# One batch-1 decode step (cached attention plus gated FFN): the rows of the down projection dealt to the partitions anew, with a part loaded by GpSimd

## The chip, the cores and the metric

The kernel runs on one core of a Trainium2 chip. The metric is the device time of one execution in microseconds (us), the median of several runs; lower is better. A profile of one further execution stands beside it. The engines are TensorE (PE, with weight loads as PEld), VectorE (DVE), ScalarE (ACT), GpSimd (POOL) and SyncE (SP). Sixteen transfer engines move data between HBM and the 128 partitions of SBUF; SP, ACT and POOL can issue transfers to them.

## The reference

One token's row `x` (576 wide) goes through a layer norm, and then through two branches whose results are added to `x`: attention over a cache of 16,384 keys with 32 heads of 128, and a feed-forward block with a gated GELU and 4,608 hidden values.

```python
x = A_x                                     # (1, 1, 576)
xn = layernorm(x)
q = (xn @ wq)                               # 32 heads x 128
scores = einsum("bhqd,bhkd->bhqk", q, k_cache) * 128 ** -0.5   # k_cache (1, 32, 16384, 128)
o = einsum("bhqk,bhkd->bhqd", softmax(scores), v_cache)
attention = o.reshape(1, 1, 4096) @ wo
h = gelu_tanh(xn @ w_gate) * (xn @ w_up)    # 4608 wide
return x + attention + h @ w_down
```

Everything is fp32. K and V are 8.4 MB per head each; with the weights the kernel reads 587.6 MB.

## The kernel before

Every large load is issued by SP, in program order, and each goes to all 128 partitions. Two SBUF slots (`kslot`) hold K tiles, one (`vslot`) holds a V tile, each 64 KB per partition. A load waits until its slot has been read by its last user.

Start: wq and the two FFN input matrices (w_gate, w_up) are loaded into the same slots. `project` multiplies the normalized row with one of them. The output columns are cut into four quarters, one for each group of 32 PSUM partitions, and into three chunks (`FB`, in columns) for the three PSUM banks; quarter q writes partitions 32q to 32q+31. In `ffn`, each of the 32 partitions of a quarter keeps its own share of the columns: a multiplication with the mask `same` (L176) and a sum (L179) leave 36 values per partition (`WD_T`) in `gu`. `ffn_act` turns them into `hT`, 128 partitions by 36 columns: partition p holds the hidden values 36p to 36p+35.

Middle: 32 heads. For head h, `qk` multiplies the K tile with the spread query (L215) and sums over 128 (L216) on VectorE; `softmax` works on 128 by 128 scores; `pv` multiplies with the V tile on TensorE (L236, 64 instructions), one head behind. SP's order is K of head h+1, then V of head h. The V of the last head goes to a `kslot`.

End: `load_rows` loads wd as 36 rows per partition in two pieces (`WD_PIECES`, 28 into the V slot `ta`, 8 into the K slot `tb`), and wo as 32 rows per partition in six pieces (`WO_PIECES` 16, 8, 4, 2, 1, 1; the first into `tb` behind wd, the others into `te`). A row is 576 values, 2,304 bytes. `add_out` multiplies one column of `hT` (wd) or `oT` (wo) with one such row across the partitions (L281): as two halves of 288, accumulated in PSUM, for wd and the first 24 rows of wo, as four quarters of 144 for the last 8 rows. After 28 rows of wo, VectorE adds both halves to `x2`, TensorE brings them into the quarters, and the last four rows follow. One copy and one store of 4 partitions by ACT's queue end the program.

GpSimd has no transfers before; it sets constants at the start.

Of the kernel before, what the change touches and what calls it, by code (L numbers as in the profile page):

```python
# [8 lines left out]
F32 = mybir.dt.float32  # L9
AF = mybir.ActivationFunctionType  # L10
ALU = mybir.AluOpType
AX = mybir.AxisListType

P = 128
H, SK, DH = 32, 16384, 128
D, DF = 576, 4608
# [3 lines left out]
DM = P * DJ  # L20
# [3 lines left out]
HD = H * DH  # L24
QG, QB = HD // 4, 512
QS = HD // 2
WD_T = DF // P
FG = DF // 4
FB = (11 * WD_T, 11 * WD_T, 10 * WD_T)
WO_T = HD // P  # L30
WD_PIECES = (28, 8)
WO_PIECES = (16, 8, 4, 2, 1, 1)
WO_A = 16
WO_Q = 8
QUART = D // 4
HG = 4
# [5 lines left out]
def kernel(ctx: ExitStack, tc: tile.TileContext, x, k_cache, v_cache, wq, wo, wg, wu, wd, out):  # L42
    nc = tc.nc
    cpool = ctx.enter_context(tc.tile_pool(name="cpool", bufs=1))
# [12 lines left out]
    wmain = {n: w[:DM].rearrange("(p j) f -> p (j f)", j=DJ) for n, w in (("q", wq), ("g", wg), ("u", wu))}  # L57
    wtail = {n: w[DM:].rearrange("d (s f) -> (d s) f", s=2) for n, w in (("q", wq), ("g", wg), ("u", wu))}
    wov = wo.rearrange("(p t) f -> p (t f)", t=WO_T)
    wdv = wd.rearrange("(p t) f -> p (t f)", t=WD_T)  # L60

    def kslot():
        return kpool.tile([P, R * DH], F32, tag="k", name="kslot")

    def vslot():
        return vpool.tile([P, R * DH], F32, tag="v", name="vslot")

    def load(dst, src):
        nc.sync.dma_start(dst, src)  # L69
        return dst  # L70

    ROW3 = 3 * DF
    wq_t, wg_t, mix = kslot(), kslot(), vslot()
    qt = load(wg_t[:, ROW3 : ROW3 + QS], wtail["q"])
    load(wq_t, wmain["q"])
    row3, tails, at = {}, {}, 0
# [2 lines left out]
        tails[n] = load(mix[:, at + DF : at + DF + DF // 2], wtail[n])  # L79
        at += DF + DF // 2  # L80

    xrow = mix[:1, ROW3 + FG : ROW3 + FG + D]
    nc.scalar.dma_start(xrow, xf)
    x2 = cpool.tile([P, HALF], F32, name="x2")
    nc.gpsimd.memset(x2, 0.0)
# [5 lines left out]
    ones = cpool.tile([P, P], F32, name="ones")  # L91
# [5 lines left out]
    same = cpool.tile([P, 32], F32, name="same")  # L97
# [14 lines left out]
    px = ps_s.tile([P, 512], F32, tag="sm", name="px")  # L112
    xm = xrow[:, :DM].rearrange("o (p j) -> o j p", j=DJ)
    for j in range(DJ):
        nc.tensor.matmul(px[:, j : j + 1], xm[:, j, :], ones[:1, :1], start=True, stop=True)
    xd = mix[:1, ROW3 + 2 * FG : ROW3 + 2 * FG + 2 * (D - DM)].rearrange("o (d s) -> o d s", s=2)
    nc.vector.tensor_copy(xd, xrow[:, DM:].unsqueeze(2).to_broadcast([1, D - DM, 2]))
    nc.tensor.matmul(px[:, DJ : DJ + 1], xd.rearrange("o d s -> o (d s)"), ones[:1, :1], start=True, stop=True)
    xp = cpool.tile([P, DJ + 1], F32, name="xp")
# [1 line left out]
    xnb = cpool.tile([P, DJ, 32], F32, name="xnb")  # L121
# [3 lines left out]
    xtb = cpool.tile([P, 2, 32], F32, name="xtb")  # L125
    nc.vector.tensor_copy(xtb, xt.unsqueeze(2).to_broadcast([P, 2, 32]))

    def project(steps, group, sizes):
        pg = ps_big.tile([P, 3, 512], F32, tag="pb", name="pg")
        for k, (j, rhs) in enumerate(steps):  # L130
            for b, size in enumerate(sizes):
                for q in range(4):
                    lo = q * group + sum(sizes[:b])
                    if j < DJ:
                        lhs = xnb[:, j, :]
                    else:
                        lhs = xtb[:, q // 2, :]
                        lo -= q // 2 * 2 * group
                    nc.tensor.matmul(pg[32 * q : 32 * q + 32, b, :size], lhs, rhs[:, lo : lo + size],  # L139
                                     start=k == 0, stop=k == len(steps) - 1)  # L140
        return pg

    steps = [(DJ, qt)] + [(j, wq_t[:, j * HD : (j + 1) * HD]) for j in range(DJ)]
    pq = project(steps, QG, (QB, QB))[:, :2, :]
    qrow = cpool.tile([P, QG], F32, name="qrow")
    nc.scalar.activation(qrow.rearrange("p (b f) -> p b f", f=QB), pq, AF.Copy)

# [2 lines left out]
    def q_spread(h):  # L150
        r = 32 * (h // (H // 4))
        lo = h % (H // 4) * DH
        pq = ps_s.tile([P, 512], F32, tag="sm", name="pq")
        nc.tensor.matmul(pq, ones[r : r + 1, :], qrow[r : r + 1, lo : lo + QH * DH], start=True, stop=True)  # L154
        return pq
# [4 lines left out]
        for i in range(QH):  # L160
            Q[h + i] = qs[:, i : i + 1, :]

    gu = cpool.tile([P, 2, WD_T], F32, name="gu")

    def ffn(which):
        n = "gu"[which]
        t = kslot() if which else wg_t
        steps = [(3, row3[n]), (DJ, tails[n])]
        load(t[:, :ROW3], wmain[n][:, :ROW3])
        steps += [(j, t[:, j * DF : (j + 1) * DF]) for j in range(DJ - 1)]  # L170
        pg = project(steps, FG, FB)
        gm = mix[:, ROW3 : ROW3 + FG].rearrange("p (m t) -> p m t", t=WD_T)
        at = 0
        for b, size in enumerate(FB):
            m = size // WD_T
            nc.vector.tensor_mul(gm[:, at : at + m, :], pg[:, b, :size].rearrange("p (m t) -> p m t", t=WD_T),  # L176
                                 same[:, at : at + m].unsqueeze(2).to_broadcast([P, m, WD_T]))
            at += m
        nc.vector.tensor_reduce(gu[:, which, :], gm.rearrange("p m t -> p t m"), axis=AX.X, op=ALU.add)  # L179

    ffn(0)
    ffn(1)

    hT = cpool.tile([P, WD_T], F32, name="hT")

    def ffn_act():
        g, u = gu[:, 0], gu[:, 1]
        t1 = cpool.tile([P, WD_T], F32, name="t1")
        tc.keep_in_program_order(nc.vector.tensor_mul(t1, g, g))
        tc.keep_in_program_order(nc.vector.tensor_scalar(t1, t1, 0.044715, 1.0, op0=ALU.mult, op1=ALU.add))  # L190
        tc.keep_in_program_order(nc.vector.tensor_mul(t1, t1, g))
        th = cpool.tile([P, WD_T], F32, name="th")
        nc.scalar.activation(th, t1, AF.Tanh, scale=0.7978845608028654)
        t2 = cpool.tile([P, WD_T], F32, name="t2")
        tc.keep_in_program_order(nc.vector.scalar_tensor_tensor(t2, th, 1.0, g, op0=ALU.add, op1=ALU.mult))
        tc.keep_in_program_order(nc.vector.scalar_tensor_tensor(hT, t2, 0.5, u, op0=ALU.mult, op1=ALU.mult))

# [51 lines left out]
    for h in range(H + 1):  # L249
        if h < H:  # L250
            KT[h], n = kslot(), R if h else SUB
            for i in range(0, R, n):
                load(KT[h][:, i * DH : (i + n) * DH], kv[h][:, i * DH : (i + n) * DH])
        if h > 0:
            VT[h - 1] = load(vslot() if h < H else kslot(), vv[h - 1])
        more = (h + 1) % QH == 0 and h + 1 < H
        pq = q_spread(h + 1) if more else None
        if h < H:
            for i in range(0, R, n):
                qk(h, i, n)  # L260
            KT.pop(h)
        if h == 0:
            ffn_act()
        if h > 0:
            pv(h - 1)
            if h % HG == 0:
                out_heads(h - HG)
        if more:
            q_take(h + 1, pq)
        if h < H:  # L270
            softmax(h)

    seen = set()
# [4 lines left out]
    def add_out(groups, lhs, w, last=False):  # L278
        n = D // len(groups)
        for i, g in enumerate(groups):  # L280
            nc.tensor.matmul(g, lhs, w[:, i * n : (i + 1) * n], start=id(g) not in seen, stop=last)  # L281
            seen.add(id(g))

    half = [[pairs[i][32 * (2 * i + j) : 32 * (2 * i + j) + 1, :HALF] for j in range(2)] for i in range(2)]
    quart = [acc4[32 * g : 32 * g + 1, :] for g in range(4)]

    def load_rows(t, at, src, lo, n):
        load(t[:, at * D : (at + n) * D], src[:, lo * D : (lo + n) * D])
        return [t[:, (at + j) * D : (at + j + 1) * D] for j in range(n)]

    ta, tb, te = vslot(), kslot(), kslot()
    a, b = WD_PIECES
    wd_rows = load_rows(ta, 0, wdv, 0, a) + load_rows(tb, 0, wdv, a, b)
    wo_rows, lo = [], 0
    for n in WO_PIECES:
        wo_rows += load_rows(tb, b + lo, wov, lo, n) if lo < WO_A else load_rows(te, lo - WO_A, wov, lo, n)
        lo += n
# [13 lines left out]

    for j, w in enumerate(wd_rows):
        add_out(half[j % 2], hT[:, j : j + 1], w)

    for j, w in enumerate(wo_rows):
        if j < WO_T - WO_Q:
            add_out(half[j % 2], oT[:, j : j + 1], w, last=j >= WO_T - WO_Q - 2)
            continue
        if j == WO_T - 4:
            nc.vector.tensor_add(x2[:64], x2[:64], PO[0][64:, :HALF])  # L320
            nc.vector.tensor_add(x2[:64], x2[:64], acc[:64, :HALF])
            for i, g in enumerate(quart):
                r, lo = 32 * (i // 2), i % 2 * QUART
                nc.tensor.matmul(g, ones[r : r + 1, :1], x2[r : r + 1, lo : lo + QUART], start=False, stop=False)
        add_out(quart, oT[:, j : j + 1], w, last=j == WO_T - 1)

    o4 = te[:, R * DH - 3 * HALF : R * DH - 3 * HALF + QUART]
# [30 lines left out]
```

## Time and profile before

| What | Value |
|---|---|
| Time, median of 3 runs | 1370.13 us (1369.86 to 1370.30) |
| The profiled execution's own time | 1370.16 us |
| Its span in the profile | 1368.3 us |
| VectorE busy | 1135.8 us (83%) |
| TensorE busy | 406.0 us (30%), weight loads 118.1 us |
| ScalarE, GpSimd busy | 36.5 us, 1.0 us |
| HBM read | 587.60 MB, 429 GB/s over the span |
| One `qk` of a full head on VectorE | L215 16.7 us mean, L216 16.7 us mean |
| First wd piece issued | 1308.00 us |
| wo pieces issued | from 1314.35 us, the second from about 1330 |

Times inside the profile count from the start of the span. The share of the transfer engines is a mean over all 16. A group's row names its line, engine, operation and tile, the shapes, the count, and then the busy time; in square brackets or behind the bar stands the idle time ahead of it and what ended it. The page counts packets by queue: q1 holds SP's loads, q10 ACT's, and q8 and q14 instruction loads.

### The profile page before, as it was taken

The page shows a single profiled execution, that of the slowest core. Times are in us where ns is not written, and L with a number is a line of the kernel's source. Part 1 is how long each engine was busy: PE and PEld are TensorE (multiplying, and loading weights), DVE is VectorE, ACT ScalarE, POOL GpSimd, SP SyncE. Part 2 cuts the span into 40 slices and gives each one's busy share as a digit, 9 for nine tenths or more (in the row PEclk, how much of TensorE's full clock was granted, in tenths as well). Part 3 has the DMA queues.
Part 4 walks back from the last instruction along what each step waited for, and adds up shares of the span by engine and source line. Part 5 has one row for each costly group of instructions (what it writes and reads, how often), then busy time and mean ns, then how long its engine had stood idle before and what let it go on. Part 6 is the DMA issues. An engine that isn't in the chain of part 4 may idle for free.

```text
span 1368.3 us, 6377 instructions
## 1 busy us (share of the span) xinstructions
PE 406.0 (30%) x2870; PEld 118.1 (9%) x2870; DVE 1135.8 (83%) x169; ACT 36.5 (3%) x126; POOL 1.0 (0%) x7
## 2 busy tenths in 40 slices
PE   4321233322311232323212332322213333221156
PEld 1110000100000000100000000100001000000012
DVE  1069999899888888898888888998888888988840
ACT  0000000000000000000000000000000000000000
POOL 0000000000000000000000000000000000000000
PEclk8775565565556556565566566565556555665577
DMA  9999999999999999999999999999999999999997
GB/s 404 440 425 450 430 429 430 430 435 432 437 435 429 431 430 439 432 432 435 431 436 433 433 431 430 435 432 439 435 430 430 431 432 437 438 435 428 429 428 336
DMA packets 11704, 588.00 MB, mean 430 GB/s; under 512 B 1303, under 2 KB 1309, under 8 KB 1694
## 3 DMA queue, kind: packets, MB, share of 16 engines
q1 hardware_dynamic: 11664, 587.60, 99.4%
q8 instruction: 22, 0.36, 0.1%
q14 instruction: 4, 0.03, 0.0%
q10 hardware_dynamic: 14, 0.01, 0.0%
HBM read 587.60 MB, written 0.00 MB: 429 GB/s over the span
## 4 chain that ended last, share of the span: by engine, by line
DMA 51%; DVE 46%; PE 2%; issue 0%; SPq 0%; ACT 0%; DVEq 0%
DMA kslot<-in_A_k_cache_dram 41%; DVE s L216 23%; DVE kslot L215 23%; DMA kslot<-in_A_v_cache_dram 3%; DMA kslot<-in_B_w_up_dram 3%; DMA kslot<-in_A_wo_dram 3%; DMA kslot<-in_A_wq_dram 2%; PE pg L139 1%; PE po L236 1%; DVE gu L179 0%; SPq L69 0%; PE pt L222 0%; DVE vslot L176 0%; DVE pm L220 0%; DVE nm L224 0%
## 5 line engine op out<-in xcount | busy, mean ns | idle before, releaser
L215 DVE TENSOR_TENSOR kslot<-kslot,qs 128x16384 f32<-128x16384 f32 (+1 forms) x33 | 551.3, 16705 | 88.4 <-DMA kslot<-in_A_k_cache_dram 86.9
L216 DVE TENSOR_REDUCE s<-kslot 128x128 f32<-128x16384 f32 (+1 forms) x33 | 551.2, 16703 | 3.3
L236 PE MATMUL po<-vslot,pe 128*16 128x512 f32 x1984 | 286.1, 741 | 645.0 <-DMA vslot<-in_A_v_cache_dram 645.0
L236 PEld LDWEIGHTS po<-vslot,pe 128*16 128x16 f32 x1984 | 67.3, 113 | 848.2 <-issue 848.2
L222 PE MATMUL pt<-ident,pm 128*1 128x128 f32 x32 | 11.9, 372 | 236.0 <-DVE pm L220 236.0
L176 DVE TENSOR_TENSOR vslot<-pg,same 128x396 f32<-128x396 f32 (+1 forms) x6 | 3.0, 552 | 69.1 <-PE pg L139 69.1
L139 PE MATMUL pg<-kslot,xnb 128*32 128x396 f32 (+2 forms) x208 | 23.6, 615 | 33.6 <-DMA kslot<-in_B_w_gate_dram 18.9
L228 ACT ACTIVATE nb<-pb 128x1 f32<-128x1 f32 x32 | 5.5, 171 | 812.4 <-PE pb L226 812.4
L320 DVE TENSOR_TENSOR x<-x,po 64x288 f32<-64x288 f32 x1 | 0.5, 457 | 30.8 <-PE po L281 30.8
L222 PEld LDWEIGHTS pt<-ident,pm 128*1 128x1 f32 x32 | 2.5, 79 | 259.4 <-DVE pm L220 218.5
L226 PE MATMUL pb<-nm,ones 1*128 1x1 f32 x64 | 18.1, 350 | 13.2 <-DVE nm L224 13.2
L224 DVE TENSOR_REDUCE nm<-pt 1x1 f32<-1x128 f32 x32 | 8.9, 278 | 14.9 <-PE pt L222 14.9
L226 PEld LDWEIGHTS pb<-nm,ones 1*128 1x128 f32 x64 | 15.8, 305 | 22.2 <-DVE nm L224 11.3
L154 PE MATMUL pq<-qrow,ones 1*128 1x512 f32 x16 | 15.6, 1073 | 0.0
L229 ACT ACTIVATE pe<-s,nb 128x128 f32<-128x128 f32 x32 | 12.8, 401 | 1.0
L302 DVE RECIPROCAL rl<-pl 128x32 f32<-128x32 f32 x1 | 0.4, 358 | 14.9 <-PE pl L300 14.9
L281 PE MATMUL acc<-kslot,oT 128*1 128x144 f32 (+1 forms) x112 | 10.5, 376 | 6.7 <-DMA kslot<-in_A_wo_dram 6.7
L139 PEld LDWEIGHTS pg<-kslot,xnb 128*32 128x32 f32 x208 | 7.1, 126 | 51.0 <-DMA kslot<-in_B_w_gate_dram 19.7
L241 ACT ACTIVATE o<-po 128x512 f32<-128x512 f32 x8 | 4.8, 597 | 222.0 <-PE po L236 222.0
L236 PE MATMUL po<-kslot,pe 128*16 128x512 f32 x64 | 9.6, 769 | 2.6 <-DMA kslot<-in_A_v_cache_dram 2.6
L281 PE MATMUL acc<-vslot,hT 128*1 128x288 f32 x56 | 8.6, 473 | 5.6 <-DMA vslot<-in_B_w_down_dram 5.6
L245 PE MATMUL pc<-same,o 128*128 128x4 f32 x64 | 8.4, 255 | 5.7 <-ACT o L241 5.7
(74 smaller groups left out, 109.9 us busy)
## 6 DMA issues: line engine op xcount, KB each, us to landing
kslot<-in_A_k_cache_dram SPq DMA_DIRECT2D x2, 4096.0 KB
vslot<-in_B_w_down_dram SPq DMA_DIRECT2D x1, 8064.0 KB
kslot<-in_B_w_gate_dram SPq DMA_DIRECT2D x1, 6912.0 KB, 54.0
kslot<-in_B_w_up_dram SPq DMA_DIRECT2D x1, 6912.0 KB
kslot<-in_A_wo_dram SPq DMA_DIRECT2D x1, 4608.0 KB, 39.2
vslot<-in_B_w_gate_dram SPq DMA_DIRECT2D x1, 2304.0 KB, 28.9
vslot<-in_B_w_up_dram SPq DMA_DIRECT2D x1, 2304.0 KB, 37.6
kslot<-in_B_w_down_dram SPq DMA_DIRECT2D x1, 2304.0 KB, 28.7
```

Source lines behind the costliest of these rows:

```text
L139: nc.tensor.matmul(pg[32 * q : 32 * q + 32, b, :size], lhs, rhs[:, lo : lo + size], start=k == 0, stop=k == len(steps) - 1)
L154: nc.tensor.matmul(pq, ones[r : r + 1, :], qrow[r : r + 1, lo : lo + QH * DH], start=True, stop=True)
L215: tc.keep_in_program_order(nc.vector.tensor_mul(blk, blk, Q[h].to_broadcast([P, n, DH])))
L216: nc.vector.tensor_reduce(S[h][:, i : i + n], blk, axis=AX.X, op=ALU.add)
L222: nc.tensor.transpose(pt[:1, :P], pm, ident)
L224: tc.keep_in_program_order(nc.vector.tensor_reduce(nm, pt[:1, :P], axis=AX.X, op=ALU.max, negate=True))
L226: nc.tensor.matmul(pb[:, :1], ones[:1, :], nm, start=True, stop=True)
L228: nc.scalar.activation(nb, pb[:, :1], AF.Copy, scale=SCALE)
L229: nc.scalar.activation(pe4, S.pop(h).rearrange("p (k s) -> p k s", s=4), AF.Exp, bias=nb, scale=SCALE, accum_out=lsum[:, h : h + 1])
L236: nc.tensor.matmul(PO[h // HG % 2][q : q + PW, :], pe[:, lo : lo + PW], vt[:, k * 512 : (k + 1) * 512], start=i == 0 and k < 4, stop=i == ...
L245: nc.tensor.matmul(pc[:, :HG], o4[:, j * DH : (j + 1) * DH], pick[:, j, :], start=j == 0, stop=j == 3)
L281: nc.tensor.matmul(g, lhs, w[:, i * n : (i + 1) * n], start=id(g) not in seen, stop=last)
```

## The change

wd has 4,608 rows. Before, partition p took the 36 rows 36p to 36p+35. Now each partition takes 33 (`WD_T`), rows 0 to 4,223 (`DX`), and the last 384 rows go, 12 more each (`WD_X`), to partitions 96 to 127 (`XP`).

- The 33 rows come in two SP pieces of 16 and 17. wo is cut into seven pieces, 11, 5, 8, 4, 2, 1, 1, with the first 11 in `tb`.
- The 12 extra rows come in four transfers that GpSimd issues. Transfer r goes to the 8 partitions 96+r, 100+r, ... 124+r, and each partition's 12 rows are read as two runs of 6 rows from two places of wd.
- Before, between and after these, GpSimd issues five transfers of 8-byte runs to 14, 8, 8, 8 and 10 partitions, into columns of `ta` that nothing reads.
- The FFN projections follow the new layout. Chunks are 15, 15 and 2 shares of 33 columns (495, 495, 66), with 384 columns more in the third chunk of the last quarter (450). Quarters begin at multiples of 1,056; where the tail's matrix (in two halves) is cut by a quarter's border, the matmul is split.
- `gu` and `hT` have 45 columns; for the last 12, partitions 96 to 127 get two more multiplications and two more sums per projection.
- The 12 extra rows are 12 further steps of `add_out` with 32 partitions, after the 33 others.
- The matmuls of `add_out` are kept in program order.

```diff
-WD_T = DF // P
-FG = DF // 4
-FB = (11 * WD_T, 11 * WD_T, 10 * WD_T)
+WD_T = 33
+WD_X = 12
+XP = 96
+DX = P * WD_T
+FT = WD_T + WD_X
+FG = 32 * WD_T
+FB = (15, 15, 2)
+FX = 32 * WD_X
-WD_PIECES = (28, 8)
-WO_PIECES = (16, 8, 4, 2, 1, 1)
-WO_A = 16
+WD_PIECES = (16, 17)
+WO_PIECES = (11, 5, 8, 4, 2, 1, 1)
+WO_A = 11
...
-    wdv = wd.rearrange("(p t) f -> p (t f)", t=WD_T)
+    wdv = wd[:DX].rearrange("(p t) f -> p (t f)", t=WD_T)
+    wdx = wd[DX:].rearrange("(s p t) f -> p s (t f)", s=2, t=WD_X // 2)
...
+        h = total // 2
...
-                    lo = q * group + sum(sizes[:b])
+                    lo = bases[q] + sum(sizes[q][:b])
+                    hi = lo + sizes[q][b]
                     if j < DJ:
-                        lhs = xnb[:, j, :]
+                        parts = [(xnb[:, j, :], lo, hi, 0)]
                     else:
-                        lhs = xtb[:, q // 2, :]
-                        lo -= q // 2 * 2 * group
-                    nc.tensor.matmul(pg[32 * q : 32 * q + 32, b, :size], lhs, rhs[:, lo : lo + size],
-                                     start=k == 0, stop=k == len(steps) - 1)
+                        parts = [(xtb[:, i, :], max(lo, i * h), min(hi, i * h + h), i * h) for i in range(2)]
+                    for lhs, a, e, o in parts:
+                        if a < e:
+                            nc.tensor.matmul(pg[32 * q : 32 * q + 32, b, a - lo : e - lo], lhs, rhs[:, a - o : e - o],
+                                             start=k == 0, stop=k == len(steps) - 1)
...
-        nc.vector.tensor_reduce(gu[:, which, :], gm.rearrange("p m t -> p t m"), axis=AX.X, op=ALU.add)
+        nc.vector.tensor_reduce(gu[:, which, :WD_T], gm.rearrange("p m t -> p t m"), axis=AX.X, op=ALU.add)
+        gx = mix[XP:, ROW3 + FG : ROW3 + FG + FX].rearrange("p (s m t) -> p s m t", s=2, t=WD_X // 2)
+        px = pg[XP:, 2, FB[2] * WD_T : FB[2] * WD_T + FX].rearrange("p (s m t) -> p s m t", s=2, t=WD_X // 2)
+        for i in range(2):
+            nc.vector.tensor_mul(gx[:, i], px[:, i], same[XP:, :].unsqueeze(2).to_broadcast([32, 32, WD_X // 2]))
+            nc.vector.tensor_reduce(gu[XP:, which, WD_T + i * WD_X // 2 : WD_T + (i + 1) * WD_X // 2],
+                                    gx[:, i].rearrange("p m t -> p t m"), axis=AX.X, op=ALU.add)
...
-            nc.tensor.matmul(g, lhs, w[:, i * n : (i + 1) * n], start=id(g) not in seen, stop=last)
+            tc.keep_in_program_order(nc.tensor.matmul(g, lhs, w[:, i * n : (i + 1) * n], start=id(g) not in seen, stop=last))
...
-    wd_rows = load_rows(ta, 0, wdv, 0, a) + load_rows(tb, 0, wdv, a, b)
+    wd_rows = load_rows(ta, 0, wdv, 0, a)
+    at = (a + WD_X) * D
+    halves = wd.rearrange("p (s f) -> p s f", s=2)
+    for r, n in enumerate((14, 8, 8, 8, 10)):
+        tc.keep_in_program_order(nc.gpsimd.dma_start(ta[0 : 4 * n : 4, at + 4 * r : at + 4 * r + 4], halves[:n, :, :2]))
+        if r < 4:
+            tc.keep_in_program_order(nc.gpsimd.dma_start(ta[XP + r : P : 4, a * D : at], wdx[r::4]))
+    wd_rows += load_rows(tb, 0, wdv, a, b)
+    wd_x = [ta[XP:, (a + j) * D : (a + j + 1) * D] for j in range(WD_X)]
...
     for j, w in enumerate(wd_rows):
         add_out(half[j % 2], hT[:, j : j + 1], w)
+    for j, w in enumerate(wd_x):
+        add_out(half[j % 2], hT[XP:, WD_T + j : WD_T + j + 1], w)
```

## The prediction

> **What bounds the kernel now.** I read the page from the top, then the chain of waits, then windows and timeline of the last 25 us, then the packets themselves.
>
> ```profile
> span 1368.3 us, 6377 instructions
> ...
> DMA  9999999999999999999999999999999999999997
> ...
> q1 hardware_dynamic: 11664, 587.60, 99.4%
> q8 instruction: 22, 0.36, 0.1%
> q14 instruction: 4, 0.03, 0.0%
> ```
>
> The transfer engines are busy in every slice but the last; the load queue alone fills 99.4% of them. VectorE (83%) has a 3.1 us gap per head. So the time is bytes over rate, plus what happens at the two ends. The chain ends in the loads of wo:
>
> ```profile
> 1318.24 9.66 PE po L236 x64
> 1329.71 35.08 DMA kslot<-in_A_wo_dram
> ```
>
> The windows of the end (us, busy time of each engine, granted clock, mean share of the 16 transfer engines, GB/s) show that the 16 do not stop together:
>
> ```profile
> 1356.00:1358.00 2.00, 2.00 (x24) 0.67 (x20) 0.00 (x0) 0.00 (x0) 0.00 (x0) 0.61 0.97 406
> 1358.00:1360.00 2.00, 2.00 (x40) 0.78 (x36) 0.00 (x0) 0.00 (x0) 0.00 (x0) 1.00 0.88 349
> 1360.00:1361.00 1.00, 1.00 (x24) 0.41 (x20) 0.00 (x0) 0.00 (x0) 0.00 (x0) 1.00 0.58 228
> 1361.00:1362.00 1.00, 0.61 (x12) 0.06 (x5) 0.32 (x1) 0.00 (x0) 0.00 (x0) 1.00 0.52 203
> 1362.00:1363.00 1.00, 0.98 (x32) 0.74 (x32) 0.58 (x2) 0.00 (x0) 0.00 (x0) 1.00 0.43 171
> 1363.00:1364.00 1.00, 1.00 (x32) 0.41 (x24) 0.00 (x0) 0.00 (x0) 0.00 (x0) 1.00 0.37 138
> 1364.00:1365.00 1.00, 0.70 (x21) 0.21 (x16) 0.00 (x0) 0.00 (x0) 0.00 (x0) 1.00 0.04 16
> ```
>
> From 1360 on about half are out of work, the last runs to 1364.4. The unused share from 1358 to 1364.36 is 0.24 + 0.42 + 0.48 + 0.57 + 0.63 + 0.32 = 2.66 us: **perfect evening gains no more than that**.
>
> The packet records tell who is late. On one engine a packet starts where the last ended, so 16 chains can be followed (a few swaps are possible). A 64 KB packet takes 2.42 us on all of them (27.07 bytes per ns). The 22 instruction packets of 16 KB visit eight engines in turn; each makes that engine's next load packet start 1.0 us late and run 0.5 us longer, 1.5 us in all. The eight have two or three such visits and their last load packets end at about 1362.5 (two) and 1363.7 to 1364.36 (six). The other eight end at 1359.1 to 1360.2, but for one at 1361.35, which takes two of the four 8 KB packets of q14 (0.97 us each). The engine that carries ScalarE's one-partition loads of x is one of the early eight. TensorE's end stands hard behind the landings:
>
> ```profile
> 1353.73 0.65 PE L281 MATMUL acc<-kslot,oT 128*1 128x288 f32 x2 [6.00 <-DMA kslot<-in_A_wo_dram]
> ...
> 1361.68 0.46 DVE L320 TENSOR_TENSOR x<-x,po 64x288 f32<-64x288 f32 x1 [30.80 <-PE po L281]
> ...
> 1363.46 1.06 PE L281 MATMUL acc<-kslot,oT 128*1 128x144 f32 x24
> ...
> 1364.83 0.42 PE L281 MATMUL acc<-kslot,oT 128*1 128x144 f32 x8 [0.30 <-DMA kslot<-in_A_wo_dram]
> ```
>
> The last row waited only 0.30 us for its load. Two things are nearly critical together: the latest engine, and TensorE's work from the 8-row piece of wo on.
>
> **The change part by part.** *Loads.* A row of wd in one partition is 2304 bytes: 0.0851 us of an engine. SP's pieces fall from 36 rows to 33; an engine serves 8 partitions (128 over 16), so each loses 24 rows, 2.04 us. The four GpSimd transfers bring 12 rows to 8 partitions each. Where a transfer of few partitions goes is seen in one row only: the output store of four partitions is four 576-byte packets of 31 to 34 ns that start within 60 ns and overlap, one engine per partition. By that, eight engines get four partitions, 48 rows, 4.08 us; net +2.04 us on eight, -2.04 us on eight. Fixed costs: two 9216-byte packets (0.351 us each) against one of 18432 (0.689) make 0.013 us a packet. The seventh piece of wo adds 8 packets, 0.10; the GpSimd transfers 8, 0.10; nine completion marks of about 0.012 with the 8-byte packets, 0.15. So +2.36 us on the eight that get the rows, -1.8 on the others. What a GpSimd packet costs no row shows. Lower bound: its bytes, 0.51 us (ScalarE's 1152-byte packets cost their engine 49 ns, close to the bytes' 43). Upper bound: the instruction packet's 1.5 us per 16 KB, 1.27 us for 13,824 bytes, 6 us more per engine. I take the lower: like ScalarE's, these move data from HBM to SBUF.
>
> *Which eight.* No row shows it. If the early ones: these end at 1361.5 to 1362.6, the one with two q14 packets at 1363.7; the late ones at 1361.9 to 1362.55. The last landing moves from 1364.36 to 1363.7: **-0.65 us**. If late ones are among them: 1364.36 + 2.36 = 1366.7, **+2.36**. I take the early ones, on an assumption that only the sizes in the diff support: that each GpSimd transfer takes the next engines in line, as many as it has partitions. Then 14, 8, 8, 8, 10 and four times 8 make 80, five rounds of 16, each real transfer begins 16 places after the last, and all four meet the same eight engines, as many as each group has. The Trainium skill (DMA: Bandwidth & Descriptors, section "Why a DMA increments its semaphore by 16 and not by 1") says that such a transfer takes consecutive engines from a cursor that moves on, but also that some direct copies from GpSimd are spread one partition per engine from engine 0, whatever went before. By the first the small transfers steer and the sum is -0.65; by the second they steer nothing, and it could be +2.36 (second rival). No run so far shows either.
>
> *GpSimd's queue.* Nine transfers, with nothing behind them but the end of the program. The first waits for the V slot, as SP's first wd piece does (issued 1308.00). The last waits for the first one's completion. The rows are needed after SP's 33, landed near 1340. Even 2.5 us for each of nine (the store's whole wait at the end) is 23 us, 1331: covered. Without cover, TensorE would stand before wo.
>
> *SP's queue.* The same waits on slots; its last one-row piece now waits for the first wd piece (about 1329): covered until 1362; only the end stands behind it.
>
> *Projections.* Four column quarters run side by side, so a step lasts as its widest: 495+495+450 = 1440 columns for 396+396+360 = 1152, a quarter more.
>
> ```profile
> 59.59 8.13 PE L139 MATMUL pg<-kslot,xnb 128*32 128x396 f32 x72 [18.88 <-DMA kslot<-in_B_w_gate_dram]
> ...
> 76.05 6.01 PE L139 MATMUL pg<-kslot,xnb 128*32 128x396 f32 x72 [2.58 <-DMA kslot<-in_B_w_up_dram]
> ```
>
> That is +1.5 to 2.0 us each, and four small VectorE operations each, 1.3 us by the rows of L176 and L179 scaled to 192 columns. K of head 1 (issued about 82) and V of head 0 (85.8) go out 2 to 4 us later, but the engines hold K of head 0 until 92.7 and K of head 1 until 112. VectorE starts head 0 3 us later; K of head 2, issued 120.7, then about 124, is needed at 131. Hidden; without cover, 3 us.
>
> *TensorE's end.* wd costs 45 rows for 36, 9 x 0.243 = 2.2 us, in stretches where TensorE waited for loads (6.00 us before 1353.73). wo comes as 11, 5, 8 for 16, 8, so TensorE is idle some 3 us before the 8-row piece. Rows took 0.48 us at clock 0.50 (1353.7 to 1357.5) and 0.243 at 1.00. The 8 rows landed at 1358.67 and would at 1358.0: at full clock they are done by 1360.6 and the landing decides, -0.65; at half clock they end near 1362.3 and the last row starts at 1365.1, +0.3. The Trainium skill (TensorE: Matmul & The Clock Gate, "Part 1: The HAM clock gate (the "warmup" mystery)") gives an idle window of about 3.4 us as what halves the clock; by that 3 us is just too short and the sum has no term here. The trace does not bear it out to the letter: its clock record falls at 1272.24, 2.5 us after TensorE stopped at 1269.8. I take most of the rows at full clock, +0.15.
>
> Sum: 1368.3 - 0.65 + 0.15 = 1367.8 span. The profiled execution took 1370.16, 1.86 outside its span, and lies within 0.03 of the median 1370.13: **1369.6 us**.
>
> **Rivals.** *All even and clock held*: the q14 packets visit other engines, or all wo rows run warm. For it: packet visits hang on code that has changed. Last landing 1362.6: 1370.13 - 1.8 = 1368.3. *The rows fall on late engines* (the other side): one engine with three instruction visits among the eight decides it. For it: a first transfer of 14 sets the start, and where zero lies no row tells; 8 of 16 engines are wrong. Against: the arithmetic above. Price +2.36 by the landing, to +3.3 where TensorE's clock has fallen too: 1372.5 to 1373.4. *TensorE's clock*: half clock for the 8 rows eats the gain, 1370.4. For it: the clock fell after 2.5 us idle at 1272. Against: the idle stretch is about 3 us. *GpSimd packets as dear as instruction packets*: 1362.6 + 6.0 = 1368.6, +4.3: 1374.4. Against: ScalarE's small packets are not.
>
> **How the numbers follow.** Forecast 0.38 (its own range 1368.8 to 1370.2), all even 0.12, TensorE's clock 0.10, late engines 0.36, dear packets 0.04. The range 1368.1 to 1373.3 leaves out the dear packets and the upper edge of the late engines. 0.2% (2.74 us) is about what a measurement of this kernel can tell from no change. Faster than 1367.39 would need more than the 2.66 us of perfect evening: 0.03 for what I may have missed. Slower than 1372.87: 0.26 of the late engines' 0.36 and the dear packets' 0.04, 0.30. The rest, 0.67.
>
> **What would show it.** In the windows of the last 6 us the transfer share should stay near 1 to about 1361 and then fall within 2 us; a share near 0.5 from 1358 to 1366 would be the late engines, and the forecast wrong. The four GpSimd transfers should land before 1331. The clock at the 8-row piece of wo, and the wait ahead of the last row (over 0.30: the landing decides; none: TensorE), tell the third rival. SP's first waits should still end before the engines run dry: a first-100-us share below today's would break the cover of the projections. 64 KB packets should still take 2.42 us.

## The result: 1375.56 us, 5.5 us slower, and the profile after

| | Before | After |
|---|---|---|
| Time, median (range) | 1370.04 us (1369.86 to 1370.30) | 1375.56 us (1375.30 to 1375.92, 6 runs) |
| Ratio to before, 95% interval | | 1.0040 [1.0030, 1.0051] |
| The profiled execution's own time / span | 1370.16 / 1368.3 us | 1375.92 / 1374.1 us |
| Last load packet ends | 1364.36 us | 1369.94 us |
| Last matmul ends | 1365.25 us | 1371.04 us |

The forecast was 1369.6 with a range to 1373.3: wrong in sign and outside its range. Last landing (+5.58), last matmul (+5.79) and span (+5.8) moved together, so the loss is in the loads of the end. The head of the page of the changed kernel, and the end of its chain of waits (start, length, what was waited for):

```profile
span 1374.1 us, 6485 instructions
...
DMA  9999999999999999999999999999999999999997
...
q1 hardware_dynamic: 11808, 586.72, 99.2%
q0 software_dynamic: 352, 0.89, 0.2%
```

```profile
1317.16 8.97 PE po L253 x64
1326.53 38.23 DMA kslot<-in_A_wo_dram
```

The transfer engines are as busy as before, with the same bytes, but the last wait on wo is 3.15 us longer (38.23 for 35.08). Busy for longer with the same bytes means slower packets. The windows say when (us, busy time of PE, PEld, DVE, ACT and POOL, clock, transfer share, GB/s). First the kernel before, then the changed kernel:

```profile
1310.00:1320.00 10.00, 2.72 (x15) 1.05 (x19) 4.51 (x3) 0.67 (x3) 0.00 (x0) 0.66 1.01 435
1320.00:1330.00 10.00, 9.15 (x70) 2.99 (x62) 0.09 (x1) 0.77 (x2) 0.00 (x0) 0.83 1.02 440
1330.00:1340.00 10.00, 3.39 (x26) 1.34 (x30) 0.75 (x3) 0.20 (x1) 0.00 (x0) 0.51 0.94 403
1340.00:1350.00 10.00, 7.73 (x124) 2.78 (x116) 0.00 (x0) 0.00 (x0) 0.00 (x0) 0.97 1.00 429
```

```profile
1310.00:1320.00 10.00, 3.79 (x19) 1.33 (x23) 1.34 (x3) 0.66 (x3) 0.61 (x2) 0.50 0.98 340
1320.00:1330.00 10.00, 7.78 (x64) 2.87 (x56) 0.84 (x3) 0.97 (x3) 0.00 (x0) 0.95 1.03 346
1330.00:1340.00 10.00, 6.91 (x64) 2.05 (x64) 0.00 (x0) 0.00 (x0) 0.00 (x0) 0.66 1.02 359
1340.00:1350.00 10.00, 1.51 (x16) 0.52 (x20) 0.00 (x0) 0.00 (x0) 0.00 (x0) 0.57 0.94 345
...
1356.00:1358.00 2.00, 2.00 (x36) 0.68 (x32) 0.00 (x0) 0.00 (x0) 0.00 (x0) 1.00 1.00 430
...
1365.00:1366.00 1.00, 1.00 (x16) 0.37 (x12) 0.00 (x0) 0.00 (x0) 0.00 (x0) 0.68 0.73 290
1366.00:1368.00 2.00, 2.00 (x20) 0.66 (x16) 0.00 (x0) 0.00 (x0) 0.00 (x0) 0.50 0.22 88
1368.00:1369.00 1.00, 1.00 (x24) 0.68 (x20) 0.58 (x2) 0.00 (x0) 0.00 (x0) 0.61 0.12 46
1369.00:1370.00 1.00, 1.00 (x32) 0.44 (x28) 0.32 (x1) 0.00 (x0) 0.00 (x0) 1.00 0.11 41
```

For forty microseconds the share is about 1 and the rate 340 to 359 GB/s, where the kernel before moved 403 to 440 in the same windows. By 1356 the rate is back (430). From 1366 to 1370 a share of 0.22 to 0.11 says that some two to four of the 16 engines still run.

The packet records show the same packet by packet. The unhindered length of each size is that of a run in which nothing slowed it:

| Packet | Unhindered | Before, mean | After, mean (range) |
|---|---|---|---|
| 65,536 (K, V after 1290) | 2418 ns | 2422.6 | 2466 (2418 to 3489) |
| 39,168 (wd, 17 rows) | 1448 | – | 1785 (1448 to 2382) |
| 36,864 (wd, 16 rows) | 1364 | – | 1702 (1364 to 2619) |
| 25,344 (wo, 11 rows) | 940 | – | 1042 (940 to 1707) |
| 13,824 (GpSimd's) | 516 | – | 678 (516 to 939) |
| 18,432 | 686 | 690.7 | 686 |

With eight packets of each wd and wo size per engine and 8.6 of 65,536 this is 8 x (337 + 338 + 102) ns + 8.6 x 48 ns = 6.6 us per engine, on engines with extra rows and without alike, as far as the chains can be told apart. Packets are long only while GpSimd's are under way (1311 to 1346), but for one that meets an instruction packet.

GpSimd issued without trouble (start, length, idle time ahead):

```profile
1305.42 0.70 POOL L314 DMA_DIRECT2D vslot<-in_B_w_down_dram  x1 [1303.84 <-PE po L253]
...
1309.48 0.56 POOL L316 DMA_DIRECT2D vslot<-in_B_w_down_dram  x1
1316.23 0.57 POOL L314 DMA_DIRECT2D vslot<-in_B_w_down_dram  x1 [6.18 <-DMA vslot<-in_B_w_down_dram]
```

The end of TensorE (the last rows of wo) shows a second effect:

```profile
1364.81 0.41 PE L298 MATMUL acc<-kslot,oT 128*1 128x288 f32 x2 [3.21 <-DMA kslot<-in_A_wo_dram]
...
1367.62 0.70 PE L298 MATMUL acc<-kslot,oT 128*1 128x288 f32 x2
...
1369.88 1.16 PE L298 MATMUL acc<-kslot,oT 128*1 128x144 f32 x32
```

TensorE waited 3.21 us for the 8-row piece; soon the clock fell to 0.50 and a matmul took 0.70 us for 0.41. The last four rows then ran without a wait.

### The profile page after: what moved, and what is told of

Its sections match the earlier page's. It is cut to its first block, busy times and chain, and to the rows that moved or that the text cites. A ratio compares the mean times of both kernels' runs of the same rounds, so it can differ in the third digit from the quotient of the medians.

```text
span 1374.1 us, 6485 instructions
## 1 busy us (share of the span) xinstructions
PE 416.8 (30%) x2910; PEld 123.1 (9%) x2910; DVE 1138.5 (83%) x178; ACT 36.5 (3%) x126; POOL 6.2 (0%) x16
## 4 chain that ended last, share of the span: by engine, by line
DVE 48%; DMA 45%; PE 4%; another core or an unknown queue 1%; issue 1%; ACT 0%; SPq 0%; DVEq 0%
DMA kslot<-in_A_k_cache_dram 37%; DVE s L233 24%; DVE kslot L232 24%; DMA kslot<-in_A_v_cache_dram 3%; PE pg L149 3%; DMA kslot<-in_A_wo_dram 3%; DMA kslot<-in_A_wq_dram 2%; PE po L253 1%; PE acc L298 0%; PE pt L239 0%; DVE gu L190 0%; DVE pm L237 0%; DVE vslot L187 0%; DVE nm L241 0%
## 5 line engine op out<-in xcount | busy, mean ns | idle before, releaser
L187 DVE TENSOR_TENSOR vslot<-pg,same 128x495 f32<-128x495 f32 (+1 forms) x6 | 2.8, 519 | 74.1 <-PE pg L149 74.1
L149 PE MATMUL pg<-kslot,xnb 128*32 128x495 f32 (+3 forms) x208 | 29.1, 643 | 28.7 <-DMA kslot<-in_B_w_gate_dram 17.0
L298 PE MATMUL acc<-vslot,hT 128*1 128x288 f32 (+1 forms) x56 | 10.0, 523 | 2.6 <-DMA vslot<-in_B_w_down_dram 2.6
```

Of the source, the lines that this page charges most:

```text
L149: nc.tensor.matmul(pg[32 * q : 32 * q + 32, b, a - lo : e - lo], lhs, rhs[:, a - o : e - o], start=k == 0, stop=k == len(steps) - 1)
L298: tc.keep_in_program_order(nc.tensor.matmul(g, lhs, w[:, i * n : (i + 1) * n], start=id(g) not in seen, stop=last))
```

## The experiments

Three theories stood against each other: (a) the rows fall on engines that were late anyway; (b) GpSimd's transfers are dear in themselves; (c) the place where the rows are written slows all loads. All kernels here compute the whole result. The first four shared 24 runs of before (1370.20), the next four 24 (1370.09), the next three 13 (1370.08), the last 11 (1370.06).

**data_only: without the five small transfers.**

```diff
-    for r, n in enumerate((14, 8, 8, 8, 10)):
-        tc.keep_in_program_order(nc.gpsimd.dma_start(ta[0 : 4 * n : 4, at + 4 * r : at + 4 * r + 4], halves[:n, :, :2]))
-        if r < 4:
-            tc.keep_in_program_order(nc.gpsimd.dma_start(ta[XP + r : P : 4, a * D : at], wdx[r::4]))
+    for r in range(4):
+        tc.keep_in_program_order(nc.gpsimd.dma_start(ta[XP + r : P : 4, a * D : at], wdx[r::4]))
```

> The changed kernel without its five small transfers; the four GpSimd transfers of the extra rows stay. In the changed kernel's trace load packets on every engine are stretched while the 13,824-byte GpSimd packets are in flight, and only then. Theory A (the rows' own GpSimd packets cost it, by their queue or by where they write): the transfer rate between 1310 and 1350 still falls to about 350 GB/s while they move; if they now take another set of eight engines, the last landing is up to 3 us earlier; 1371 to 1375. Theory B (the small transfers and their completion marks cost it): the rate stays near 430 and the time is 1369 to 1371.

Measured: 1371.48 us (1371.22 to 1372.08), ratio 1.0010 [1.0000, 1.0019]. Now the four transfers alternate between two groups of eight engines, and the records contrast them inside one kernel: packets of the first (starting near 1310 to 1315) take up to 1081 ns and of the third (1320 to 1327) up to 894; of the second (1316 to 1319) and fourth (from 1327.9) 516 to 534. The same rows at the same partitions cost their bytes' price from one eight and more from the other. That speaks against (b) and for (c).

**sp_four: the four transfers issued by SP, GpSimd does nothing.** In place of the GpSimd loop:

```diff
+    for r in range(4):
+        load(ta[XP + r : P : 4, a * D : at], wdx[r::4])
```

> The same four transfers of eight partitions, issued by SP behind the first wd piece; nothing from GpSimd, no small transfers. Theory A1 (GpSimd's queue is what is dear): no stretched packets, 1368 to 1370.5, depending on which eight engines SP's transfers take. Theory A2 (the destination is what is dear: partitions 96 to 127 are written by engines that otherwise write other partitions): the same stretch as with GpSimd, 1372 to 1375. Theory B (small transfers): as A1.

Measured: 1376.55 us (1374.24 to 1377.07), ratio 1.0043 [1.0028, 1.0058]: as slow without GpSimd, so (b) falls. Nine in ten of the 13,824-byte packets take over 0.9 us (mean 1022 ns, longest 1119): twice 516. Of the 128 packets of 39,168 bytes 31 take 2.7 to 3.1 us, about twice 1.448, 18 lie between, and 79 keep 1.448. Windows of this kernel:

```profile
1310.00:1320.00 10.00, 6.10 (x31) 1.83 (x35) 1.25 (x3) 0.67 (x3) 0.00 (x0) 0.51 1.02 437
1320.00:1330.00 10.00, 6.24 (x56) 2.63 (x44) 0.84 (x3) 0.97 (x3) 0.00 (x0) 0.83 1.09 244
1330.00:1340.00 10.00, 5.67 (x64) 1.73 (x64) 0.00 (x0) 0.00 (x0) 0.00 (x0) 0.83 0.89 312
1340.00:1350.00 10.00, 3.18 (x28) 0.99 (x32) 0.00 (x0) 0.00 (x0) 0.00 (x0) 0.51 0.98 423
```

The rate falls to 244 GB/s at a full share just while these packets run (1321 to 1334).

**deal_one: the rows in one SP transfer to the 32 partitions.** In place of the GpSimd loop:

```diff
+    load(ta[XP:, a * D : at], wdx)
```

> The new dealing with the extra rows in one SP transfer to partitions 96 to 127, two partitions to each engine if it is spread over all 16; so no shift between the engines and nothing from GpSimd. All theories but A2: the projections, the seven pieces of wo and TensorE's extra rows are hidden, the last landing is where it was, 1370 to 1370.6. A2: packets stretched for some microseconds, 1372 to 1374.

Measured: 1373.46 us (1372.84 to 1374.65), ratio 1.0025 [1.0015, 1.0035]. The packets are as long (mean 1026 ns), 233 GB/s from 1320 to 1330. By the chains they now lie on all 16 engines, about four each, so no engine has more rows than before; with (a) out of the way, 1373.46 - 1366.67 = 6.8 us over the kernel before at the same slot offset (pad_224 below) is left for (c). The changed kernel less gp_low is 6.8 us too (below), but with packets of another length on eight engines, so that the two agree so closely is in part chance.

**small_only: the kernel before with the five small transfers alone.**

```diff
+    for r, n in enumerate((14, 8, 8, 8, 10)):
+        tc.keep_in_program_order(nc.gpsimd.dma_start(ta[0 : 4 * n : 4, at + 4 * r : at + 4 * r + 4], halves[:n, :, :2]))
```

> The kernel before with the five small GpSimd transfers alone, rows dealt as before. Theory B: 3 to 6 us more, 1373 to 1376. Theory A: under 0.6 us, about 1370.3, with no stretched packets but at the small packets themselves.

Measured: 1370.30 us (1370.16 to 1370.49), ratio 1.0001 [0.9991, 1.0010]. The tiny transfers cost nothing that can be told.

**sp_low: the same rows on partitions 0 to 31, by SP.**

```diff
-XP = 96
+XP = 0
+XE = XP + 32
...
+    for r in range(4):
+        load(ta[XP + r : XE : 4, a * D : at], wdx[r::4])
```

`FT`, `hT` and the twelve steps stay; the 384 columns of the projections go to the first quarter, where a matmul with zeros opens the accumulation and the two stretches of columns follow.

> The new dealing with the extra rows on partitions 0 to 31 for 96 to 127, in four SP transfers of eight partitions; nothing from GpSimd. Where SP's transfers of eight partitions to 96 to 127 ran at half rate (1040 ns for 516) and doubled other engines' packets, theory A2 says that each engine writes the partitions it always serves at full rate, and that two engines share one path when one writes the other's partitions. If SP's eight engines serve partitions 0 to 63, no packet is stretched here (13,824 bytes in 516 ns, 39,168 in 1448), the late engines end 2 us sooner, the early ones 2.3 later: the time is 1365.5 to 1367.5 with the shorter 64 KB packets (2418 ns) that all kernels of the new layout show. Rival A3, any extra transfer of few partitions is dear wherever it writes: stretched packets as before, 1372 to 1376.

Measured: 1368.32 us (1367.29 to 1368.61), ratio 0.9986 [0.9976, 0.9995]. Every 13,824-byte packet takes 516 ns. The windows of this kernel:

```profile
1320.00:1330.00 10.00, 8.12 (x72) 3.35 (x68) 0.84 (x3) 0.97 (x3) 0.00 (x0) 0.84 1.00 432
1330.00:1340.00 10.00, 5.32 (x56) 1.49 (x48) 0.00 (x0) 0.00 (x0) 0.00 (x0) 0.67 0.94 405
```

The same transfers, rows and issuing engine as in sp_four, 8.2 us apart: only the partitions differ, with the projections that lead to them. This settles (c) for SP. What is left of (a) is seen too: the engines that carry rows and take three instruction packets end at 1362.31 and 1362.43, those with three and no rows at 1358.7 to 1359.0.

**gp_low: the same by GpSimd, each transfer followed by a small one of 8 partitions.**

```diff
+        tc.keep_in_program_order(nc.gpsimd.dma_start(ta[XP + r : XE : 4, a * D : at], wdx[r::4]))
+        tc.keep_in_program_order(nc.gpsimd.dma_start(ta[0:32:4, at + 4 * r : at + 4 * r + 4], halves[:8, :, :2]))
```

> The same rows on partitions 0 to 31, issued by GpSimd, each of the four transfers followed by a small one of eight partitions, so that all four fall on the same eight engines. A2: no stretch beyond the packets' own switching, within 1.5 us of the SP version, 1365.5 to 1369. Theory A1 (GpSimd's queue is dear in itself): stretched load packets between 1310 and 1350 on all engines, 3 us or more above the SP version.

Measured: 1368.77 us (1368.22 to 1369.76), ratio 0.9989 [0.9980, 0.9999]. All 64 packets take 516 ns. Windows of this kernel:

```profile
1320.00:1330.00 10.00, 8.12 (x96) 3.47 (x88) 0.84 (x3) 0.97 (x3) 0.00 (x0) 1.00 1.03 441
1330.00:1340.00 10.00, 1.47 (x27) 0.44 (x22) 0.00 (x0) 0.00 (x0) 0.00 (x0) 0.79 0.95 406
```

With GpSimd as issuer, and with the small transfers, the median is 0.45 us over SP's. The last landings differ by 0.36 us (1362.79 and 1362.43), and the runs of the two overlap, so a cost of the issuer is small at most.

**pad_224 and after_pad_32: a hidden gain.** The larger constants of the changed kernel move the K and V slots in SBUF: they began at byte 27,680 of a partition, 32 past a multiple of 256, and begin at 27,904, a multiple of 256. One kernel gives the kernel before this offset by an unused tile that is set to zero, the other takes it away from the changed kernel in the same way.

```diff
+    pad = cpool.tile([P, 56], F32, name="pad")   # before
...
+    pad = cpool.tile([P, 8], F32, name="pad")    # after
```

> The kernel before with a constant tile of 224 bytes per partition more, so that the K and V slots begin where they do in the changed kernel (SBUF offset 27,904 per partition, a multiple of 256, for 27,680, 32 above a multiple of 64). All kernels of the new layout show 64 KB packets of 2418 ns for 2420 to 2428. If the offset is the reason: 512 packets per engine times 4.6 ns, 2.4 us less, 1367.5 to 1368.2. If it is something else in the new layout: 1370.0 to 1370.4.

> The changed kernel with 32 bytes more per partition ahead of the slots (offset 27,936, again 32 above a multiple of 64). If the offset shortens the packets: 64 KB packets of 2420 to 2428 ns again and about 2.4 us more than the changed kernel, 1377.5 to 1378.5. Otherwise 1375.3 to 1375.9.

Measured: pad_224 1366.67 us (1366.46 to 1366.96), ratio 0.9975 [0.9965, 0.9984]; after_pad_32 1378.84 us (1378.61 to 1380.12), ratio 1.0065 [1.0050, 1.0080]. The offset is worth 3.4 us before and 3.3 after. At equal offset the change costs 1378.84 - 1370.09 = 8.75 us at the old one and 1375.56 - 1366.67 = 8.89 at the new. After 1290 every 64 KB packet takes 2418 ns in pad_224, in the kernel before 2419 to 2428 (mean 2422.6).

**who: which engines take instruction packets.** pad_224 with eight tiny SP loads to 1, 2, ... 8 partitions, each with its own packet size, so that an engine is known by the sizes that it carries.

```diff
+    for k in range(1, 9):
+        n = 22 + k
+        load(ta[0 : 4 * k : 4, at : at + n], wd[:k, :n])
+        at += n
```

> A reading, not a timing: the kernel before at the slots' better offset, with eight tiny SP loads more behind the first wd piece, of 1, 2, 3 ... 8 partitions and of a size of their own (92 to 120 bytes a partition), so that the packet records tell which chain is the first engine, the second and so on. If the eight engines that SP's transfers of eight partitions take are all early ones, none of the eight chains takes an instruction packet of 16 KB; the version with the rows on partitions 0 to 31 ended with two engines late, so I expect that two of the eight take them. SP's waits on its completion counters will cost a few microseconds: 1367 to 1373.

Measured, in a single run: 1371.4 us; the engines ran dry for 2.4 to 6.6 us near 1330 while SP issued these loads. The load of k partitions goes to the first k engines. As far as the chains can be told apart, engines 0 to 4 and 7 take no instruction packets, while 5 and 6 take two or three; the other six late ones then lie among 8 to 15. So the early eight are not eight in line: any eight in line include a late engine.

**sp_64 and sp_32: the other two places.** sp_low with another `XP`.

```diff
-XP = 0
+XP = 64    # or 32
```

> The extra rows on partitions 64 to 95 for 0 to 31, by the same SP transfers, nothing else changed. Theory A2 (two engines share one path where one writes partitions that the other serves): as on 96 to 127, half rate (13,824 bytes in about 1040 ns) and stretched wd packets, 1374 to 1377. Rival A4 (only the last quarter is slow, or the earlier version's layout): full rate, 1367.5 to 1369.

> The same on partitions 32 to 63. Theory A2, with engine i of the first eight serving 4i to 4i+3 and 32+4i to 32+4i+3: full rate, 516 ns, as on 0 to 31, 1367.5 to 1369. Rival A4' (only the first quarter is fast): half rate, 1374 to 1377.

Measured: sp_64 1377.54 us (1375.45 to 1378.83), ratio 1.0053 [1.0038, 1.0068]; sp_32 1368.73 us (1367.51 to 1372.22), ratio 0.9992 [0.9982, 1.0001]. The 13,824-byte packets: mean 1029 ns on 64 to 95, all 516 on 32 to 63. Windows of sp_64:

```profile
1320.00:1330.00 10.00, 7.25 (x64) 2.70 (x54) 0.84 (x3) 0.97 (x3) 0.00 (x0) 0.97 1.08 253
1330.00:1340.00 10.00, 6.31 (x64) 1.89 (x64) 0.00 (x0) 0.00 (x0) 0.00 (x0) 0.66 0.95 256
```

Upper half of the partitions slow, lower half not. The Trainium skill ("SBUF — State Buffer", section "Door 1: The DMA port swizzle (why `[64,N]` ≈ `[32,N]`)") says that eight partitions share one of 16 ports, 0 to 63 on eight of them and 64 to 127 on the other eight; "DMA: Bandwidth & Descriptors" (section "The descriptor swizzle") that a 128-partition transfer gives each engine one port, engines 0 to 7 the lower partitions. The four places agree: where engines 0 to 7 write the lower half, nothing slows; where they write the upper half, two engines write one port, and packets take 1022 to 1029 ns for 516. The records don't name ports, so that it is the port is an inference; that it hangs on engine and partition together is shown, by the four places and by data_only.

**four_engines: the rows where they cost nothing.** If this is so, rows should go to engines without instruction packets, on partitions of their own: 0 to 15 for engines 0 to 3. sp_low with 35 rows for all and 8 more for these, at the good offset.

```diff
-WD_T = 33
-WD_X = 12
-XE = XP + 32
+WD_T = 35
+WD_X = 8
+XE = XP + 16
...
-WD_PIECES = (16, 17)
-WO_PIECES = (11, 5, 8, 4, 2, 1, 1)
+WD_PIECES = (20, 15)
+WO_PIECES = (13, 3, 8, 4, 2, 1, 1)
```

> Slots at offset 27,904 as in pad_224; each row block of wd keeps 35 rows for all 128 partitions and gives partitions 0 to 15 eight rows more, by four SP transfers of 4 partitions, one for each of the engines 0 to 3, which take no instruction packets and serve these partitions. Theory (engines that write partitions of their own keep their rate, the two- and three-visit engines set the last landing): those lose 8 rows of 2 KB for each partition, 0.68 us by the price in the prediction, engines 0 to 3 gain 24 rows net, 2.04 us, on ends 4 us earlier; no packet stretched (13,824-byte packets absent, the 39,168-byte ones' successors at their bytes' price); 1365.8 to 1366.5 against pad_224's 1366.67. Rival, TensorE's half clock at the end decides by now: last landing earlier by 0.5 to 0.7 us, but the time stays at 1366.5 to 1368. Rival, the shared path costs also where the engine writes its own partitions: 1370 or more.

Measured: 1366.13 us (1365.91 to 1366.22, 7 runs), ratio 0.9971 [0.9959, 0.9982]: the lowest median of the study, 3.9 us under before and 0.54 under pad_224, whose own runs began at 1366.46. Load packets keep their unhindered lengths but for the few that meet an instruction packet. The last landing is 1360.47, where pad_224 has 1361.25: 0.78 earlier for the 0.68 expected. The timeline of this kernel's last row:

```profile
1360.84 0.42 PE L309 MATMUL acc<-kslot,oT 128*1 128x144 f32 x8 [0.28 <-DMA kslot<-in_A_wo_dram]
```

It waited 0.28 us for its load, at full clock: the landing decides.

## Why the prediction was wrong

The 5.5 us come out as: offset of the slots -3.4 (pad_224), rows on eight engines in line that include late ones +2.1 (gp_low less pad_224), packets slowed at the upper partitions and what follows from them +6.8 (after less gp_low). The offset was not in the prediction, the late engines were its second rival, the slowed packets were missing.

By the last landings of the profiled executions the three terms are -3.1, +1.5 and +7.2, 5.6 together. So the 2.1 is not late engines alone. In gp_low TensorE waited 3.84 us for the 8-row piece and then worked at half clock, and its last matmul ends 2.10 us after the last landing, where pad_224 has 0.81 and the changed kernel 1.10. That execution is the slowest of its ten. A window of gp_low, clock 0.50:

```profile
1360.00:1361.00 1.00, 1.00 (x12) 0.29 (x8) 0.00 (x0) 0.00 (x0) 0.00 (x0) 0.50 0.14 55
```

- **Loads, "I take the lower: like ScalarE's, these move data from HBM to SBUF".** This step failed. A packet was priced by its bytes, whatever partition it writes and whichever engine carries it. In gp_low the price was right to the nanosecond (516 ns, 0.51 us forecast): GpSimd's packets are not dear. At partitions 96 to 127 they took 678, and made others longer: 6.6 us per engine, a term that the sum lacked. "GpSimd packets as dear as instruction packets" came near in time (1374.4) by luck, with a mechanism that sp_four and gp_low refute.
- **The price of rows**, 4.08 us between an engine with and one without: sp_low shows 3.3 to 3.7 between engines with three visits (1362.31 to 1362.43 against 1358.73 to 1359.00). Right in kind, a little large. The packet sums do not close fully: for the late engine 2.36 + 6.6 + 8 x 0.162 for its own rows - 3.1 (landing of pad_224 against before) = 7.2, and its landing moved by 5.58. The chains of that stretch cannot all be told apart, and the rest stays open.
- **Which eight.** The arithmetic of places held: of the small transfers' packets the engines with rows carry one each and the others five, just what eight places in line give when the count runs on through 14, 8, 8, 8, 8, 8, 8, 8, 10. So the Trainium skill's rule of a cursor that moves on, weighed there, agrees with the trace; all transfers starting at engine 0 does not. What failed is "if the early ones": the early eight are not in line (who), and the late-engines rival came true for two engines (in the changed kernel they end at 1369.74 and 1369.94, all others by 1367.13).
- **GpSimd's queue**: nine issues of 0.56 to 0.70 us, the last 6.18 us after the one before, all out by 1316.8. The extra rows landed by 1346.3, not 1331. By then SP's wd pieces were still landing (39,168-byte packets start until 1346.5), so the cover was thin, but it held.
- **Projections**: the step over w_gate took 10.34 us for 8.13, 2.2 us more for the 1.5 to 2.0 forecast, and was hidden: the first 120 us moved 405, 439 and 444 GB/s, for 404, 438 and 445.

```profile
59.03 10.34 PE L149 MATMUL pg<-kslot,xnb 128*32 128x495 f32 x72 [16.98 <-DMA kslot<-in_B_w_gate_dram]
```

- **TensorE's end.** "Most of the rows at full clock" failed: after a wait of 3.21 us most of the 8 rows ran at half clock. The last landing was so late that this cost only some 0.2 to 0.3 us: from the last landing to the last matmul it is 1.10 us, for 0.89 before and 0.81 in pad_224. In sp_low, where landings end at 1362.43, the same clock (0.51 from 1358 to 1360) puts the last matmul 1.03 us behind, in gp_low 2.10 and in sp_32 2.32: the third rival is real there.
- **"64 KB packets should still take 2.42 us"** was a test, and 2418 for 2422.6 ns passed it. But the difference matters: over the whole run the means are 2423.9 ns before and 2419.9 in pad_224, and 64 tiles of K and V are 512 such packets per engine, 512 x 4.0 ns = 2.0 us of the 3.4; where the rest lies was not followed up. The Trainium skill ("DMA: Bandwidth & Descriptors", section "How a descriptor splits into AXI transactions") says of reads that a descriptor which does not start at a multiple of 256 bytes begins with a transaction at the multiple below and pays for the unused bytes. Here it is the written side that moved; the trace agrees in sign and puts it at 0.2% for 64 KB.

## What to carry to other kernels

Before rows are dealt to idle transfer engines, ask which partitions each engine writes in the large loads: here engines that wrote others' partitions slowed the others' packets as well as their own. A transfer share near 1 with fewer GB/s is the sign to look for, and the lengths of equal-sized packets in the records then tell whose path is shared. When an edit changes the size of constants, look where the large buffers begin, and compare at equal offsets: here a gain of 3.4 us covered a good third of a loss of 8.8.

## What the runs showed of the hardware that was not expected

- Transfers of 0.89 MB, of 587.6 in all, can take a fifth of the core's load rate for forty microseconds: 340 to 359 GB/s for 403 to 440.
- SP's packets on a shared path take twice their length while a quarter of one load's packets take theirs twice too (sp_four); GpSimd's in the changed kernel take 1.3 times theirs while the loads of all engines, as far as told apart, get longer by less. Why the two share differently was not tried.
- 32 bytes in the offset of a buffer move this kernel by 3.3 us (after_pad_32).
- TensorE's clock halved after shorter pauses than thought: after a wait of 3.21 us in the changed kernel and of 3.13 us in sp_low, each 0.5 to 0.8 us into the work that followed. The prediction had cited the Trainium skill's 3.4 us as what halves it; these two pauses were shorter. In every trace here the clock record keeps a state for whole multiples of 3.41 us, and in the 3.41 us that end at these two falls TensorE was busy for 0.55 and 0.79 us: a pause need not fill that stretch.
- Each 16 KB instruction packet goes to one of eight engines, and those finish last in the kernel before by up to 5.2 us (1364.36 against 1359.12). Four engines without them took 24 rows more on balance (four_engines) and the end still came 0.78 us earlier.
